# Chunks 5 and 6 rounded behind attention, set differences on VectorE split over the first three steps, sums of weights rounded one a unit from unit 2 on

## The chip, the cores and the metric

The kernel runs on one core of a Trainium2 chip. The metric is the device time of one execution in microseconds (us), as the median of several runs. Engines: TensorE (PE), VectorE (DVE), ScalarE (ACT), GpSimd (POOL), and SyncE (SP), whose queue issues nearly all transfers here.

## What is computed

Retention attention over q, k, v of shape (2, 8, 768, 64), and then two feed-forward layers over the 1536 tokens of width 512, with 2048 hidden features each; the first with SiLU, the second with a leaky ReLU, all in float32:

```python
def _attn_ref(q, k, v):
    gamma = 1.0 - 2.0 ** (-5.0 - np.arange(H))
    for t in range(S):
        state = gamma[None, :, None, None] * state + np.einsum('bhd,bhe->bhde', k[:, :, t], v[:, :, t])
        y[:, :, t] = (1.0 / np.sqrt(D)) * np.einsum('bhd,bhde->bhe', q[:, :, t], state)
def reference(...):
    x = attn_out.transpose(0, 2, 1, 3).reshape(B * S, H * D)
    h = x @ moe_w_in;  x = (h * sigmoid(h)) @ moe_w_out
    h = x @ moe2_w_in; return np.maximum(0.01 * h, h) @ moe2_w_out
```

## The kernel before, in words

**Precision.** Every float32 operand is split into a rounded high half (ScalarE copies it to fp32r) and the rest (VectorE subtracts: L200 and L201 in `halves`). A product is three matmuls: high by high, high by low, low by high. Weights come from DRAM as 64-bit words; `words`, `clamp`, `sign` and `low` make a float32 block of them (ScalarE L144, L146; VectorE L150, L154, L161, L168). The block lies in one of three buffers `r`; `u` holds the low words. A block that is used later is stored to DRAM scratch (`keep_w`, `scr`) and fetched again (`fetch_w`).

**Attention.** Twelve chunks of 128 tokens, two at a time: scores (L266), masked scores on VectorE (L273), values (L283), the product with the state (L295), the outer product (L309) and the new state (L322). `store_x` takes a chunk's result from PSUM and splits it. Three chunks form a set of 384 tokens. Set 0 is split into `xa[0]`, set 1 into a borrowed buffer `b12[0]` and `xb[0]`, sets 2 and 3 likewise for the second pair. The unsplit values stay in `xf` (even sets) and `tm` (odd sets); for the first six chunks (`LATE`) VectorE writes them there scaled, and the split reads them from there. `amid` and `behind` hold the weight work placed inside and after each pair of chunks; `wa`, `wb`, `wc`, `wd` are the first four weight blocks of layer 0.

**Up projections.** Each layer has eight steps (`Q`); a step makes two blocks of 128 hidden features for all tokens. The first two steps of layer 0 and the first of layer 1 are plain products (L878). The others use a seven-product Strassen scheme (`rest`, L394) on token pairs of sets: `first_t` and `rest_t` form the differences of the sets, `split_t` splits them into `T4` (tiles tt), and `sums` forms the sums of weight blocks in `sf`, which `split_s` splits. ScalarE copies partial products out of PSUM (L426) and VectorE adds (L430). `up_tasks` says which helper work is issued ahead of which product. A step's results `g` are kept in DRAM (`keep`, L445); two `big` buffers take turns.

**Down projections.** In layer 0, `fetch_g` (L459) and `split_g` bring g back and `down` (L471) multiplies; each unit is one of the eight pieces of hidden features for one set of 512 tokens. In layer 1 class `Two` does it: units 0 to 7 are plain (L586), the other 32 use seven products (L602) and need the sums of the second weights, which `keep_s` formed in `u` and stored (`scrs`); `ask` fetches them (L576) into `sf` and `u` by turns, and ScalarE and VectorE split them (L648, L654). `third` splits the weights of units 2 to 7 into tiles wt; `high` and `left` (L555, L559) split g.

**Order.** There is no scheduler: the order on each engine, and on SP's transfer queue, is that in which the code issues.

## Time and profile before

| | before |
|---|---|
| median of 3 runs | 560.4 us (559.39 to 563.42) |
| profiled execution | 561.33 us, of which the span is 559.5 us |
| TensorE busy | 542.5 us, 97% of the span |
| VectorE busy | 417.6 us, 75% |
| ScalarE busy | 301.8 us, 54% |
| GpSimd busy | 104.7 us, 19% |
| transfers | 127.54 MB, mean 228 GB/s |

The profile is one execution; times in its rows are microseconds from the start of the span. Busy shares are means over the whole span. Where TensorE waits is read from the list of waits and the timeline. By place: attention runs to about 51 us, the up projection of layer 0 to 173, its down projection to 304, the up projection of layer 1 to 426, and the last stage (class `Two`) to the end.

### The profile page before, as it was taken

Reading aid. Unit: us, or ns where it says so; the run is one execution under the profiler, and the core shown is the slowest. Engines: PE = TensorE matmul, PEld = TensorE weight load, DVE = VectorE, ACT = ScalarE, POOL = GpSimd, SP = SyncE. Lnnn points to the kernel's source line nnn. Section 1 sums busy time; section 2 is a strip of 40 time slices with the busy share of each in tenths; the row PEclk is TensorE's granted clock in tenths of the full one; section 3 lists DMA queues with packets and bytes.
Section 4 is the critical chain, followed back from the end, with each engine's and each line's share of the span. In section 5 each row is a group of like instructions: output and inputs, shape, how many; then the busy total and the mean of one; then the engine's idle time right before and its main releaser. Section 6 shows DMA issues by size and latency. Waiting matters only on the chain.

```text
span 559.5 us, 8890 instructions
## 1 busy us (share of the span) xinstructions
PE 542.5 (97%) x3546; PEld 503.0 (90%) x3546; DVE 417.6 (75%) x546; ACT 301.8 (54%) x367; POOL 104.7 (19%) x92
## 2 busy tenths in 40 slices
PE   7989999999999999999999999998999979999996
PEld 6878999999998788888888999998999858999996
DVE  3798787999956687664867677767877278898993
ACT  2135586777774566644445376646765166443440
POOL 2585322333300000000600662202200000000000
PEclk8999999999999999999999999999999989999999
DMA  8982335778767977889274427776747986642521
GB/s 319 406 336 78 137 127 193 281 266 283 256 227 266 406 237 241 251 289 293 83 255 164 183 114 301 294 293 223 281 150 258 382 311 220 197 136 77 183 82 39
DMA packets 41789, 127.54 MB, mean 228 GB/s; under 512 B 3730, under 2 KB 12050, under 8 KB 39700
## 3 DMA queue, kind: packets, MB, share of 16 engines
q1 hardware_dynamic: 41456, 126.63, 63.8%
q8 instruction: 28, 0.46, 0.3%
q10 hardware_dynamic: 292, 0.34, 0.2%
q14 instruction: 13, 0.11, 0.1%
HBM read 85.01 MB, written 41.94 MB: 227 GB/s over the span
## 4 chain that ended last, share of the span: by engine, by line
PE 58%; DVE 17%; DMA 11%; ACT 5%; issue 5%; POOL 2%; SPq 1%; DVEq 0%; ACTq 0%; POOLq 0%
PE p L394 12%; PE b L394 9%; PE b L602 8%; PE p L471 6%; PE b L471 6%; PE p L602 6%; DMA scr<-r 4%; PE b L878 3%; DVE w L201 3%; DMA c<-g 2%; PE p L878 2%; PE p L586 2%; DVE r L168 2%; PE b L586 2%; DMA sf<-scrs 2%
## 5 line engine op out<-in xcount | busy, mean ns | idle before, releaser
L394 PE MATMUL p<-tt,w 128*128 128x384 f32 x468 | 87.9, 335 | 2.2 <-ACT c L426 2.2
L394 PEld LDWEIGHTS p<-tt,w 128*128 128x128 f32 x468 | 81.8, 188 | 2.9 <-ACT c L426 2.8
L471 PE MATMUL b<-w,wt 128*128 128x512 f32 x216 | 55.1, 390 | 0.5 <-DVE wt L201 0.5
L471 PE MATMUL p<-w,wt 128*128 128x512 f32 x216 | 54.8, 389 | 0.0
L201 DVE TENSOR_TENSOR w<-c,w 128x1024 fp32r<-128x1024 f32 x23 | 29.7, 1293 | 28.9 <-ACT w L200 28.9
L146 ACT ACTIVATE u<-ws 128x1024 int32<-128x1024 uint32 x32 | 36.5, 1139 | 26.3 <-DVE r L168 26.2
L426 ACT ACTIVATE c<-p 128x768 f32<-128x768 f32 x39 | 31.5, 811 | 32.4 <-PE p L394 27.1
L471 PEld LDWEIGHTS b<-w,wt 128*128 128x128 f32 x216 | 40.4, 188 | 9.4 <-DVE wt L201 1.1
L197 POOL TENSOR_TENSOR sf<-r 128x256 f32<-128x256 f32 x26 | 27.7, 1087 | 110.4 <-DVE r L168 59.8
L471 PEld LDWEIGHTS p<-w,wt 128*128 128x128 f32 x216 | 40.5, 188 | 8.4
L161 DVE SCALAR_TENSOR_TENSOR r<-ws,r 128x1024 int32<-128x1024 int32 x32 | 44.3, 1386 | 0.8
L144 ACT ACTIVATE r<-ws 128x1024 f32<-128x1024 f32 x32 | 36.5, 1140 | 13.6 <-DMA scr<-r 7.9
L430 DVE TENSOR_TENSOR big<-b,c 128x384 f32<-128x384 f32 x78 | 39.6, 550 | 5.0 <-ACT c L426 4.6
L168 DVE CUSTOM_DVE_ANT_0 r<-r,u 128x2048 uint16<-128x2048 uint16 x32 | 40.3, 1261 | 0.9
L200 ACT ACTIVATE w<-c 128x1024 fp32r<-128x1024 f32 x23 | 24.4, 1060 | 21.5 <-DMA c<-g 21.5
L201 DVE TENSOR_TENSOR w<-sf,w 128x1024 fp32r<-128x1024 f32 x14 | 17.1, 1225 | 23.3 <-ACT w L200 23.3
L154 DVE TENSOR_SCALAR r<-r 128x1024 int32<-128x1024 int32 x32 | 30.1, 940 | 1.1
L150 DVE TENSOR_SCALAR r<-r 128x1024 f32<-128x1024 f32 x32 | 24.7, 771 | 7.7 <-ACT r L144 7.7
L201 DVE TENSOR_TENSOR w<-r,w 128x768 fp32r<-128x768 f32 (+1 forms) x19 | 22.0, 1159 | 9.9 <-ACT w L200 9.9
L394 PE MATMUL b<-tt,w 128*128 128x384 f32 x156 | 29.2, 335 | 0.0
L394 PE MATMUL p<-xa,w 128*128 128x384 f32 x156 | 29.1, 335 | 0.0
L394 PE MATMUL b<-xb,w 128*128 128x384 f32 x156 | 29.1, 335 | 0.0
(178 smaller groups left out, 1129.7 us busy)
## 6 DMA issues: line engine op xcount, KB each, us to landing
ws<-w_dram SPq DMA_DIRECT2D x64, 512.0 KB, 5.5
g<-big SPq DMA_DIRECT2D x15, 1536.0 KB, 6.9
c<-g SPq DMA_DIRECT2D x30, 512.0 KB, 7.3
att_t<-att_dram SPq DMA_DIRECT2D x20, 512.0 KB, 8.6
scr<-r SPq DMA_DIRECT2D x18, 512.0 KB, 5.9
r<-scr SPq DMA_DIRECT2D x18, 512.0 KB, 5.8
c<-g SPq DMA_DIRECT2D x17, 256.0 KB, 3.4
scrs<-u SPq DMA_DIRECT2D x8, 512.0 KB, 4.0
```

The lines of the kernel that those rows point to most:

```text
L144: nc.scalar.activation(out=r.bitcast(F32), in_=t[:, :, :, 1].bitcast(F32), func=AF.Abs)
L146: nc.scalar.activation(out=u, in_=t[:, :, :, 0].bitcast(U32), func=AF.Copy, scale=2.0 ** -29)
L154: nc.vector.tensor_scalar(out=r, in0=r, scalar1=3, scalar2=0x3FFFFFF8, op0=ALU.logical_shift_left, op1=ALU.bitwise_and,)
L161: nc.vector.scalar_tensor_tensor(out=r, in0=t[:, :, :, 1], scalar=-0x40000000, in1=r, op0=ALU.bitwise_and, op1=ALU.bitwise_or)
L168: nc.vector.tensor_tensor(out=r, in0=r, in1=u, op=ALU.add)
L201: nc.vector.tensor_tensor(out=l, in0=s, in1=h.bitcast(F32), op=ALU.subtract)
L394: nc.tensor.matmul(out=o, lhsT=a[:, ta, k * 128:k * 128 + 128], rhs=rhs(p, tb, k), start=(begin and m == 0), stop=(end and m == 5), skip_g ...
L426: nc.scalar.activation(out=ct[n][:, c, 0:N], in_=t[:, :, 0:N], func=AF.Copy)
L430: nc.vector.tensor_tensor(out=self.block(f, half, c), in0=t[:, :, 0:N], in1=ct[n][:, c, 0:N], op=ALU.add)
L471: nc.tensor.matmul(out=y, lhsT=l, rhs=r, start=(i == 0 and f == 0 and n == 0), stop=(i == Q - 1 and f == 1 and n == 2),)
L602: nc.tensor.matmul(out=y[at][:, 256 * half:256 * half + 256], lhsT=g[:, tg, b], rhs=w[:, tw, a] if sm is None else S[i][tw][:, sm], start= ...
L878: nc.tensor.matmul(out=y[m][0][p][:, 0:N], lhsT=a[:, ta, (A11, A21)[f] + kk // 2, k * 128:k * 128 + 128], rhs=x, start=(i == 0), stop=(i = ...
```

## The change

Six edits. Chunks at positions 4 and 5 (`LATER`, the fifth and sixth) are no longer split in `store_x`, but by `round_x` after the fifth pair of chunks; the clamp of `wb` moves behind the sixth pair. The differences of the sets and the sums of `wc` and `wd` go from GpSimd to VectorE and are dealt out over steps 0 to 2 of layer 0, with `split_t` cut into `high_t` (ScalarE) and `left_t` (VectorE); in step 0 of layer 1 the second half of the differences goes to VectorE too, and one split moves to step 1. `words` can take the buffer `r` given back last. The results of step 6 are kept before the next fetch of g, not after step 7. In layer 1 the last two weight blocks are split before their sums are formed (`direct_s`), and the second piece of g is split one task later. In `Two`, the sums' splits start at unit 2 instead of unit 1, each behind the unit's own work, and the last three are later.

```diff
+LATER = (4, 5)
...
-    def words(w, which=(0, 1)):
+    def words(w, which=(0, 1), at=0):
         t = stage[w]
         if 0 in which:
-            r = rs[w] = rt.pop(0)
+            r = rs[w] = rt.pop(at)
...
-            nc.gpsimd.tensor_tensor(out=o, in0=a, in1=b, op=op)
+            (e or nc.gpsimd).tensor_tensor(out=o, in0=a, in1=b, op=op)
...
+    def high_t(p, n):
+        t = T4[p][:, 2 * n:2 * n + 2]
+        nc.scalar.activation(out=t[:, :, 0], in_=(tm, xf)[n][p], func=AF.Copy)
+
+    def left_t(p, n):
+        t = T4[p][:, 2 * n:2 * n + 2]
+        nc.vector.tensor_tensor(out=t[:, :, 1], in0=(tm, xf)[n][p], in1=t[:, :, 0].bitcast(F32), op=ALU.subtract)
...
     def split_t(p, n):
-        t = T4[p][:, 2 * n:2 * n + 2]
-        halves(t[:, :, 0], t[:, :, 1], (tm, xf)[n][p])
+        high_t(p, n)
+        left_t(p, n)
...
             nc.vector.tensor_tensor(out=f, in0=y, in1=g4(G), op=ALU.mult)
             y = f
+        if j in LATER:
+            return
+        round_x(j, y)
+        if j >= LATE:
+            nc.scalar.activation(out=f, in_=y, func=AF.Copy)
+
+    def round_x(j, y=None):
+        s, c = divmod(j, PER)
+        a, b = c * C, c * C + C
+        if y is None:
+            y = (tm if s % 2 else xf)[s // 2][:, :, :, a:b]
...
+            SUMS = {2: (0,), 3: (1,), 4: (2,), 5: (3,), 6: (4,), 7: (5, 6), 10: (7,)}
+            ASK = {0: (0, 1), 2: (2,), 3: (3,), 4: (4,), 5: (5,), 6: (6,), 7: (7,)}
...
-                if 1 <= n <= Q:
-                    k = n - 1
+                for k in SUMS.get(n, ()):
                     nc.scalar.activation(out=S[k][0], in_=hold[k % 2], func=AF.Copy)
...
-                for k in range(2) if n == 0 else [n + 1] if n + 1 < Q else []:
+                for k in ASK.get(n, ()):
                     ask(k)
...
+        def direct_s(w):
+            t = W[w] = free.pop(0)
+            halves(t[:, 0], t[:, 1], rs[w].bitcast(F32))
+            keep_s(w)
+            rt.append(rs.pop(w))
...
-            nc.gpsimd.tensor_copy(out=gate, in_=l[:, 1, 511:512].bitcast(F32))
...
-            4: lambda: (load_next(), clamp(wb)), 5: lambda: signed(wb),
+            4: lambda: (load_next(), [round_x(j) for j in LATER]), 5: lambda: (clamp(wb), signed(wb)),
...
-                    at(0, lambda: low(wb), lambda: first_t(0, nc.gpsimd), lambda: rest_t(0, nc.gpsimd))
-                    at(1, lambda: words(wc), lambda: split_a(wb))
-                    at(2, lambda: clamp(wc), lambda: signed(wc))
-                    at(3, lambda: low(wc), lambda: sums(wc))
-                    at(4, lambda: split_t(0, 0), lambda: first_t(1, nc.vector))
-                    at(6, lambda: split_t(1, 0))
+                    at(3, lambda: low(wb), lambda: first_t(0, nc.vector))
+                    at(4, lambda: split_a(wb))
+                    at(5, lambda: rest_t(0, nc.vector), lambda: words(wc))
+                    at(6, lambda: clamp(wc), lambda: signed(wc), lambda: low(wc), lambda: split_t(0, 0))
                 else:
-                    at(0, lambda: split_t(0, 1), lambda: rest_t(1, nc.vector))
-                    at(2, lambda: split_a(wc), lambda: words(wd))
-                    at(3, lambda: split_s(wc))
-                    at(4, lambda: split_t(1, 1), lambda: clamp(wd))
-                    at(5, lambda: signed(wd))
-                    at(6, lambda: low(wd), lambda: sums(wd))
+
+                    at(0, lambda: first_t(1, nc.vector), lambda: high_t(0, 1))
+                    at(1, lambda: split_a(wc), lambda: words(wd))
+                    at(2, lambda: high_t(1, 0), lambda: rest_t(1, nc.vector), lambda: left_t(1, 0))
+                    at(3, lambda: sums(wc, nc.vector))
+                    at(4, lambda: left_t(0, 1))
+                    at(5, lambda: split_s(wc))
+                    at(6, lambda: clamp(wd), lambda: signed(wd))
+                    at(7, lambda: high_t(1, 1))
                 return t
             if layer == 0:
+                if k == 2:
+                    at(0, lambda: left_t(1, 1), lambda: low(first_w[3]), lambda: sums(first_w[3], nc.vector))
...
-                    at(4, lambda: (low(b), sums(b)), lambda: words(w, (0,)))
+                    at(4, lambda: (low(b), sums(b)), lambda: words(w, (0,), -1))
...
-                at(0, lambda: fetch_w(n), lambda: first_t(1, nc.vector), lambda: rest_t(1, nc.gpsimd))
+                at(0, lambda: fetch_w(n), lambda: first_t(1, nc.vector), lambda: rest_t(1, nc.vector))
...
-                at(7, lambda: split_t(1, 1), lambda: sums(m))
+                at(7, lambda: sums(m))
                 return t
+            if k == 1:
+                at(0, lambda: split_t(1, 1))
...
-            at(2, lambda: words(w))
+            at(2, lambda: words(w, at=-1))
...
-            at(5, lambda: (low(w), keep_s(w), direct(w) if k > 5 else keep_w(w)))
+            at(5, lambda: (low(w), direct_s(w)) if k > 5 else (low(w), keep_s(w), keep_w(w)))
...
-                    if n:
-                        before.keep()
-                    elif s.layer == 0:
-                        fetch_g(0, 0, 1)
-                    else:
-                        Two.now.fetch(1)
+                    before.keep()
+                    if n is None:
+                        fetch_g(0, 0, 1) if s.layer == 0 else Two.now.fetch(1)
...
-                    tasks[4] += [lambda: two_.fetch(2), lambda: fetch_w((1, 1, 3)), lambda: two_.round(1)]
+                    tasks[4] += [lambda: two_.fetch(2), lambda: fetch_w((1, 1, 3))]
+                    tasks[5] += [lambda: two_.round(1)]
```

TensorE's own order is the same before and after. Three places show how the other engines' orders move. (The numbers behind the names of buffers are handles; lines are those of the kernel named.)

VectorE in attention, from the scaling of the fifth chunk to the new states, before (b_328 and p_364 are PSUM tiles, w_86 and xb_66 hold the split of set 1, c the masked scores):

```order
L363 TENSOR_TENSOR big_69<-b_328,gst 128x2x2x128
L201 TENSOR_TENSOR w_86<-big_69,w_86 128x2x128
L201 TENSOR_TENSOR xb_66<-big_69,xb_66 128x2x128
L273 TENSOR_TENSOR c<-p_364,c 128x1024
L273 TENSOR_TENSOR c<-p_373,c 128x1024
L322 TENSOR_TENSOR gst<-gst,b_391 128x256 x2
```

and after, up to the words of `wa`:

```order
L371 TENSOR_TENSOR big_69<-b_327,gst 128x2x2x128
L273 TENSOR_TENSOR c<-p_363,c 128x1024
L273 TENSOR_TENSOR c<-p_372,c 128x1024
L322 TENSOR_TENSOR gst<-gst,b_386 128x256 x2
L371 TENSOR_TENSOR big_69<-b_336,gst 128x2x2x128
L150 TENSOR_SCALAR r_73<-r_73 128x1024
```

The two passes of L201 between the scaling and the masked scores are gone, and so are the two that stood between the sixth chunk's scaling and L150; all four stand behind the tenth chunk's rounding now.

ScalarE at the start of the last stage, from unit 1's weights on, before (wt are weights of units 2 to 7, gh and w_88 pieces of g, s the sums, which come in sf and u):

```order
L200 ACTIVATE w_89<-r_73 128x1024
L441 ACTIVATE big_68<-big_68 128x2x384
L200 ACTIVATE wt_3548<-r_2584 128x1024
L555 ACTIVATE gh_3563<-c 128x1024
L200 ACTIVATE wt_3548<-r_75 128x1024
L555 ACTIVATE gh_3431<-c 128x1024
L648 ACTIVATE s_3550<-sf 128x1024
L200 ACTIVATE wt_3548<-r_73 128x1024
L555 ACTIVATE w_88<-c 128x1024
L648 ACTIVATE s_3550<-u 128x1024
```

and after:

```order
L200 ACTIVATE w_88<-r_74 128x1024
L572 ACTIVATE w_87<-c 128x1024
L458 ACTIVATE big_68<-big_68 128x2x384
L200 ACTIVATE wt_3546<-r_75 128x1024
L572 ACTIVATE gh_3561<-c 128x1024
L200 ACTIVATE wt_3546<-r_2582 128x1024
L572 ACTIVATE gh_3429<-c 128x1024
L200 ACTIVATE wt_3546<-r_74 128x1024
L572 ACTIVATE w_87<-c 128x1024
L666 ACTIVATE s_3548<-sf 128x1024
```

The first split of sums (from sf) has moved behind the weights and the piece of g of unit 4; unit 1's piece of g stands behind unit 1's weights now.

SP's queue around the same place, before (g_6 is the store of step 6's results, scrs the sums of the second weights, c the fetched pieces of g):

```order
L183 DMA scrs_3399<-u 128x1024
L510 DMA c<-g_1_2827 128x2x512
L187 DMA r_2584<-scr_1_2_2451 128x1024
L510 DMA c<-g_2_2956 128x2x512
L187 DMA r_75<-scr_1_3_2762 128x1024
L183 DMA scrs_3524<-u 128x1024
L445 DMA g_6_3542<-big_69 128x3072
L510 DMA c<-g_3_3085 128x2x512
```

and after:

```order
L183 DMA scrs_3399<-u 128x1024
L462 DMA g_6_3462<-big_69 128x3072
L527 DMA c<-g_1_2825 128x2x512
L187 DMA r_75<-scr_1_2_2449 128x1024
L527 DMA c<-g_2_2954 128x2x512
L187 DMA r_2582<-scr_1_3_2760 128x1024
L183 DMA scrs_3524<-u 128x1024
L527 DMA c<-g_3_3083 128x2x512
```

The store of step 6 stands ahead of the fetch of piece 1 instead of ahead of that of piece 3. Layer 0 has the same exchange.

## Rows read from the trace of the kernel before

**Rows 1.** The page, part 1: busy us, share of the span, instructions.
```profile
PE 542.5 (97%) x3546; PEld 503.0 (90%) x3546; DVE 417.6 (75%) x546; ACT 301.8 (54%) x367; POOL 104.7 (19%) x92
```
**Rows 2.** Waits of TensorE: line and releaser, us in total, times, longest us.
```profile
PE b L283 <- DVE c L273: 2.2, 2, 1.8
PE p L394 <- ACT c L426: 2.2, 2, 1.7
PE p L586 <- ACT w L555: 2.1, 1, 2.1
PE p L586 <- DVE w L559: 1.1, 1, 1.1
...
PE b L471 <- DVE wt L201: 0.5, 1, 0.5
```
**Rows 3.** Timeline of TensorE, last stage: start, us, engine, line, operation.
```profile
426.02 1.54 PE L586 MATMUL p<-w,gh 128*128 128x512 f32 x6
...
442.48 1.53 PE L586 MATMUL p<-wt,gh 128*128 128x512 f32 x6
...
475.06 0.87 PE L602 MATMUL p<-w,gh 128*128 128x256 f32 x6
```
**Rows 4.** Busy time by stretch: length, PE, PEld, DVE, ACT, POOL, clock, DMA.
```profile
448.00:454.00 6.00, 2.74 (x7) 1.92 (x7) 5.67 (x5) 6.00 (x7) 0.00 (x0) 0.79 0.70 230
```
**Rows 5.** VectorE's groups by shape: total us, mean ns, idle before.
```profile
L201 DVE TENSOR_TENSOR xb<-big,xb 128x256 fp32r<-128x256 f32 x4 | 2.5, 624 | 0.0
...
L201 DVE TENSOR_TENSOR w<-big,w 128x256 fp32r<-128x256 f32 x3 | 2.0, 672 | 1.4 <-ACT w L200 1.4
```
**Rows 6.** The same view: the groups that price the first steps.
```profile
L161 DVE SCALAR_TENSOR_TENSOR r<-ws,r 128x1024 int32<-128x1024 int32 x32 | 44.3, 1386 | 0.8
...
L154 DVE TENSOR_SCALAR r<-r 128x1024 int32<-128x1024 int32 x32 | 30.1, 940 | 1.1
...
L201 DVE TENSOR_TENSOR w<-sf,w 128x1024 fp32r<-128x1024 f32 x14 | 17.1, 1225 | 23.3 <-ACT w L200 23.3
...
L201 DVE TENSOR_TENSOR tt<-big,tt 128x1536 fp32r<-128x1536 f32 x8 | 14.5, 1813 | 5.3 <-ACT tt L200 5.3
...
L181 DVE TENSOR_TENSOR u<-r 128x256 f32<-128x256 f32 x16 | 6.1, 422 | 0.3
...
L348 DVE TENSOR_TENSOR big<-big,big 128x768 f32<-128x768 f32 x1 | 1.0, 953 | 0.0
```
**Rows 7.** Timeline of VectorE: the last chunk's last rounding.
```profile
57.11 0.42 DVE L201 TENSOR_TENSOR xb<-b,xb 128x256 fp32r<-128x256 f32 x1 [0.45 <-ACT xb L200]
```
**Rows 8.** Chain that ended last: start, us, what; step 2's first product.
```profile
87.65 2.09 PE p L394 x12
```
**Rows 9.** Timeline of ScalarE in layer 1's up projection, idle before and releaser behind.
```profile
321.80 1.06 ACT L200 ACTIVATE w<-sf 128x1024 fp32r<-128x1024 f32 x1 [3.73 <-POOL sf L197]
...
376.46 1.12 ACT L144 ACTIVATE r<-ws 128x1024 f32<-128x1024 f32 x1 [3.76 <-DMA scr<-r]
```
**Rows 10.** Line L183, the store of u issued at 368.9: its landing.
```profile
DMA to landing us min/median/max: 6.3/6.3/6.3
```
**Rows 11.** Timeline of ScalarE in the last stage.
```profile
447.24 1.06 ACT L648 ACTIVATE s<-sf 128x1024 fp32r<-128x1024 f32 x1 [8.14 <-DMA sf<-scrs]
```
**Rows 12.** Line L187, the fetch of unit 4's weights at 434.5: its landing.
```profile
DMA to landing us min/median/max: 10.0/10.0/10.0
```
**Rows 13.** Line L459, the fetch of piece 1 at 169.0: its landing.
```profile
DMA to landing us min/median/max: 4.2/4.2/4.2
```
**Rows 14.** Timeline of ScalarE and TensorE at the start of layer 0's down projection.
```profile
174.72 1.05 ACT L200 ACTIVATE w<-c 128x1024 fp32r<-128x1024 f32 x1
...
178.36 1.52 PE L471 MATMUL b<-w,w 128*128 128x512 f32 x6
```
**Rows 15.** Line L445, the store of step 6's g at 174.7: its landing.
```profile
DMA to landing us min/median/max: 10.9/10.9/10.9
```
**Rows 16.** Timeline of VectorE at the end of attention.
```profile
51.87 2.22 DVE L154 TENSOR_SCALAR r<-r 128x1024 int32<-128x1024 int32 x1
```

More of the change, by code (lines that the diff above doesn't have):

```diff
@@ L87, in retention_moe_kernel @@
     z1 = sb.tile([128, 1], F32, name="z1")
-    gate = sb.tile([128, 1], F32, name="gate")
     one = sb.tile([1, 64], F32, name="one")
@@ L190, in blocks, with sums @@
         return rs[w].bitcast(F32).rearrange("p a (b n) -> p (a b) n", b=2)
-    def sums(w, which=range(4)):
+    def sums(w, e=None):
         A21, A22, A11, A12 = (blocks(w)[:, n] for n in range(4))
@@ L195, in sums @@
         for o, a, b, op in [((S1, A21, A22, ALU.add), (S3, A11, A21, ALU.subtract),
-                             (S2, S1, A11, ALU.subtract), (S4, A12, S2, ALU.subtract))[n] for n in which]:
-            nc.gpsimd.tensor_tensor(out=o, in0=a, in1=b, op=op)
+                             (S2, S1, A11, ALU.subtract), (S4, A12, S2, ALU.subtract))[n] for n in range(4)]:
+            (e or nc.gpsimd).tensor_tensor(out=o, in0=a, in1=b, op=op)
     def halves(h, l, s):
@@ L369, in store_x @@
             halves(*put(s, a, b, 1)[0:2], y[:, 1])
-        if j >= LATE:
-            nc.scalar.activation(out=f, in_=y, func=AF.Copy)
     TERMS = ((0, 0), (0, 1), (1, 0))
@@ L652, in run @@
                     self.left(n + 2)
-                if 1 <= n <= Q:
+                for k in SUMS.get(n, ()):
                     nc.vector.tensor_tensor(out=S[k][1], in0=hold[k % 2], in1=S[k][0].bitcast(F32), op=ALU.subtract)
-                for k in range(2) if n == 0 else [n + 1] if n + 1 < Q else []:
+                for k in ASK.get(n, ()):
                     ask(k)
@@ L802, in up_tasks @@
                 if k == 0:
-                    at(0, lambda: low(wb), lambda: first_t(0, nc.gpsimd), lambda: rest_t(0, nc.gpsimd))
-                    at(1, lambda: words(wc), lambda: split_a(wb))
-                    at(2, lambda: clamp(wc), lambda: signed(wc))
-                    at(3, lambda: low(wc), lambda: sums(wc))
-                    at(4, lambda: split_t(0, 0), lambda: first_t(1, nc.vector))
-                    at(6, lambda: split_t(1, 0))
-                else:
-                    at(0, lambda: split_t(0, 1), lambda: rest_t(1, nc.vector))
-                    at(2, lambda: split_a(wc), lambda: words(wd))
-                    at(3, lambda: split_s(wc))
-                    at(4, lambda: split_t(1, 1), lambda: clamp(wd))
-                    at(5, lambda: signed(wd))
-                    at(6, lambda: low(wd), lambda: sums(wd))
+                    at(3, lambda: low(wb), lambda: first_t(0, nc.vector))
+                    at(4, lambda: split_a(wb))
+                    at(5, lambda: rest_t(0, nc.vector), lambda: words(wc))
+                    at(6, lambda: clamp(wc), lambda: signed(wc), lambda: low(wc), lambda: split_t(0, 0))
+                else:
+                    at(0, lambda: first_t(1, nc.vector), lambda: high_t(0, 1))
[6 more added lines that the diff above has]
+                    at(7, lambda: high_t(1, 1))
                 return t
             if layer == 0:
+                if k == 2:
+                    at(0, lambda: left_t(1, 1), lambda: low(first_w[3]), lambda: sums(first_w[3], nc.vector))
                 if k + 1 < Q:
                     a = first_w[k + 1]
-                    at(0, lambda: split_a(a))
-                    at(1, lambda: split_s(a))
+                    at(int(k == 2), lambda: split_a(a))
+                    at(1 + int(k == 2), lambda: split_s(a))
                 w = second_w[0][k - 2]
@@ L951, in retention_moe_kernel @@
                 rest(s, n, steps[k - 1], tasks)
-            steps[Q - 2].keep()
             steps[Q - 1].act(0, 1)
```

## The prediction

> **What bounds the kernel now.** The page's busy shares come first: TensorE is busy for 97% of the span, VectorE for 75%, GpSimd for 19% [rows 1]. The change leaves TensorE's instruction order as it is and removes no matmul, so what it can give back is TensorE's idle time, and what slower matmuls behind an idle stretch cost. I therefore read the waits of TensorE next [rows 2]: who it waited for, the total, how often, the longest. Five waits matter. The values product of attention (L283) waits for the masked scores of VectorE (L273), 1.8 us in one piece. The Strassen products (L394) wait twice for ScalarE's copy out of PSUM (L426), 1.7 and so 0.5 us. The last stage (L586) waits 2.1 us for a rounded piece of g on ScalarE and 1.1 us more for its low half on VectorE. The first down stage (L471) waits 0.5 us. That is 7.7 us of waiting.
>
> The last stage costs more than its waits. In the timeline its unit 0 (units are counted from 0) starts at 426.02 and unit 3 at 442.48, so a unit takes 5.49 us and eight take 43.9; the next phase starts at 475.06, 49.04 after the first [rows 3]. The excess is 5.1 us, 3.2 of it the waits. The rest is slow matmuls: after the idle stretch the granted clock is 0.79 on the mean from 448 to 454 us [rows 4], that is, TensorE was put from 2.4 to 1.2 GHz for part of it.
>
> **The change part by part, in the order of the program.**
>
> *Chunks 5 and 6.* Four VectorE roundings leave the attention stage, at 0.67 and 0.62 us mean; the group also shows 1.4 us of waiting for ScalarE over three chunks, so 0.47 each [rows 5]. Two chunks are 2 x (0.67 + 0.62 + 0.47) = 3.5 us. They stand ahead of the masked scores that TensorE waits 1.8 us for, so that wait goes. The lower bound is 0 (VectorE reaches the scores before TensorE has made them), the upper 2.2, if its lead takes away as much as both waits of that row of rows 2. What is late next: the following masked scores, since TensorE now comes 1.8 us earlier and VectorE has its 3.5 us to meet that with. I take 1.7. The rounding comes back before the last two chunks are stored, 4 x about 0.42 us (the smaller passes of the same kind are below the means above), beside the first two products of step 0, which read only xa[0]. It is hidden there.
>
> *Set differences, splits and the weights' sums on VectorE.* GpSimd loses six set differences and the eight small sums of the first steps; VectorE gets them, and its order becomes a single chain from the last chunk of attention to the sums of the second weight block (wc), which step 2's first product needs. I price it by group means [rows 6]: two groups of word passes at no more than 0.94 + 0.94 + 1.39 + 1.39 = 4.66 us, 9.3; eight set differences at 0.95, 7.6; three low halves of tt at 1.81, 5.4; four sums at 0.42, 1.7; three low halves of weights at 1.23, 3.7. Together 27.7 us. It starts where the last chunk's rounding ends, 57.11 + 0.42 before [rows 7], some 1.7 earlier now: 55.8. So it ends at 83.5. TensorE begins that product at 87.65 before [rows 8], so at about 85.9 now. The margin is 2.4 us and I cost the part at nothing; if the cover goes, each us beyond 2.4 is a us of TensorE. The DMA queues keep their order here; the third block's words are asked for by signed(wb), right after attention as before.
>
> *First weights of the second layer.* With the differences of set pair 1 on VectorE, GpSimd is free for the sums of the first Strassen block, for which ScalarE waited 3.7 us before it could come to the copy that held TensorE [rows 9]. This is the 0.5 us wait; it goes.
>
> *words(w, at=-1).* It takes the buffer given back last instead of the one that is still being stored. In the second layer ScalarE stood 3.8 us before L144 for that store [rows 9], with L146, L441 and the copy L426 behind it: this is the 1.7 us wait. What ends last now is the store of u, which L146 overwrites: issued at 368.9, landed 6.3 later, at 375.2 [rows 10], 2.4 us before the 376.46 + 1.12 at which L146 could start. So the copy comes 2.2 to 2.4 us earlier and 1.7 goes. Lower bound 0, if that store takes longer in the new order.
>
> *Last stage.* ScalarE waited 8.1 us for the sums' transfer before it rounded them, and only then came to unit 4's weights and piece of g that TensorE stood idle for [rows 11]. Now the first sums come one unit later and behind both. What is late next is unit 4's own weights: asked for at 434.5 and landed 10.0 later, 444.5 [rows 12]. Two ScalarE passes (1.06 each, as the one in rows 11) and one VectorE pass (1.23, as the low half of this size in rows 6) behind it end at 447.9; the unit starts at 426.02 + 4 x 5.49 = 447.98. So the stall goes even with the old queue, and with g of step 6 stored a step earlier 1.5 MB less stand ahead of these weights. The order of ScalarE shows no other wait ahead of a unit. I take all 5.1 us, and 0 as the other bound. The last sum, rounded at unit 10, is one VectorE pass of 1.2 us in a phase where VectorE rounds two units ahead: at nothing. So is the new order at the start of the stage (unit 1's weights rounded before their sums are formed, unit 1's piece of g after them): these are the same passes, and unit 1 starts 5.49 us after unit 0.
>
> *Keeping g of step 6 before the next fetch, both layers.* In the first layer this takes 1.5 MB from in front of the pieces for unit 3, where TensorE waits 0.5 us; that wait goes. It puts them in front of unit 1's piece, which is the second rival.
>
> **Sum.** 1.7 + 0.5 + 0.5 + 1.7 + 5.1 = 9.5 us. The profiled execution took 561.3 us (span 559.5), so 551.8; the median of the runs is 0.9 below it. What was removed is waiting, and part of the 0.9 may be waiting of that one execution, so I take a third of it off and say 551.5.
>
> **Rivals.**
> *A. The last stage keeps its stall in another place.* Unit 4 has 0.1 us to spare by the old landing; if the earlier keep moves nothing forward, or the transfers of the next weights, which share the queue with the sums, are late, TensorE falls idle and the clock with it. Price up to 5.1: 556.6. Against it: 1.5 MB less are under way. Chance 0.12.
>
> *B. The keep delays unit 1.* In the first layer the fetch landed 4.2 us after its issue at 169.0 [rows 13]; ScalarE took it up at 174.72 and unit 1 began at 178.36 [rows 14]. The keep of step 6, in the crowded stretch where it stood before, took 10.9 us [rows 15]. If the fetch lands only with such a keep, it is 6.7 us later, at 179.9, 5.2 after 174.72; ScalarE and VectorE take 1.05 and 1.2 (done at 177.1, so 1.2 to spare), which leaves a stall of 4.0: 555.5. For it: both go through SP's one queue. Against it: that keep took 10.9 with weight loads ahead of it, and here it goes first into queues that have little to do. The Trainium skill speaks against the change here: "DMA: Bandwidth & Descriptors", section on queues, rings and completion order, says that each DMA engine takes the pieces of one queue in ring order, so the fetch would stand behind all of the keep. No row here shows the two queued so. By that rule, with a keep as slow as that one, the time is 555.5; by the row alone, where the fetch needed 4.2, it is 551.5. Chance 0.10.
>
> *C. Attention gives nothing.* VectorE is ahead, but the next masked scores or GpSimd's scaling of the queries hold TensorE instead: 551.5 + 1.7 = 553.2. Chance 0.10.
>
> *D. Slower: VectorE becomes the bound of the first three steps.* The 27.7 us chain meets its end with 2.4 to spare. A pass can cost far more than its mean: L154 took 2.22 us at 51.87 [rows 16], 2.4 times its mean. If the whole chain ran at 1.8 times its price, 50 us, TensorE would stand 20 us at step 2 and the time be 571; slower than before by 1% it is from 14.5 us of delay, a chain of 45 us. The 2.22 came beside GpSimd's differences, and the new order gives GpSimd nothing to do there until the fifth weight block's sums. Chance 0.04.
>
> **How the numbers follow.** The forecast has 0.64, A 0.12, B 0.10, C 0.10, D 0.04; its own range is 549.5 to 554. For the range I go down to 548.5 (the other 0.5 of the attention bound, the rest of the 0.9, and as much as the runs spread in their faster half) and up to 556.6, A in full; D and a little on either side stay out. One per cent, about what a measurement of this kernel can tell from no change, is 5.6 us: faster means below 554.8. The forecast, C and half of B lie there, 0.79; the rest of B and A are within 1%, 0.17; D is slower.
>
> **What would show it.** In the profile after: no wait of L283 for L273 above 0.5 us, and the first L878 near 49.8; no wait of L394 for ScalarE's copy; the last stage 44 us long from its first unit to the 256-column matmuls, at a granted clock of 1.00; no VectorE wait of TensorE at step 2, with the wc sums' low half ended before TensorE's product at about 86. The prediction is wrong if TensorE shows a new wait over 1 us: for VectorE between 60 and 100 us (D), for unit 1's piece in either layer (B), or for a transfer in the last stage (A).

## The result, and the profile of the changed kernel

The changed kernel takes 553.08 us in the median of 4 runs (552.97 to 554.74), beside 561.66 for the kernel before on the same chip: a ratio of 0.9856 with a 95% interval of 0.981 to 0.9902. On a second chip it was 551.82 (550.91 to 552.71) beside 559.74, again 0.9856, interval 0.9839 to 0.9873, that is 7.1 to 9.0 us less. The forecast was 551.5, in a range of 548.5 to 556.6. The profiled execution took 552.97, its span 551.2; that of before was 561.33 and 559.5, while the median of before on the three chips used later was 559.2 to 560.0. That execution of before had a mean granted clock of 0.992; of the 49 runs of before on those three chips, nine had 0.998 and took 557.0 to 559.2.

The waits of TensorE in the profile after (line and releaser, us in total, times, longest; L411 was L394, L443 was L426, L488 was L471, L603 was L586); three that stand in the profile of before too are left out:

```profile
PE p L411 <- ACT big L458: 0.7, 1, 0.7
PE b L488 <- DVE wt L201: 0.6, 1, 0.6
PE b L309 <- POOL att_w L249: 0.5, 1, 0.5
PE b L283 <- DVE c L273: 0.4, 1, 0.4
PE p L411 <- ACT c L443: 0.4, 1, 0.4
```

Against [rows 2], the 1.8 us piece for L273, the 1.7 for ScalarE's copy and both waits of the last stage are gone. The wait of the first down stage is still there, 0.6 us instead of 0.5, and 0.7 for ScalarE's activation L458, 0.5 for GpSimd's keys (L249) and 0.4 for a copy at another place (165 us) are new. The prediction had said that no wait for ScalarE's copy would be left; that sign failed, without harm to the forecast. The stretch behind unit 4 of the last stage, to be set beside [rows 4] (clock third from the end):

```profile
450.00:460.00 10.00, 10.00 (x45) 8.03 (x44) 9.22 (x14) 5.44 (x6) 0.00 (x0) 1.00 0.81 262
```

Where the stages begin on TensorE, first before (the last stage is in [rows 3]), then after:

```profile
51.55 4.46 PE L878 MATMUL p<-xa,w 128*128 128x384 f32 x24
172.88 1.55 PE L471 MATMUL b<-w,w 128*128 128x512 f32 x6
304.34 2.28 PE L878 MATMUL p<-xa,w 128*128 128x384 f32 x12
```

```profile
47.46 4.45 PE L905 MATMUL p<-xa,w 128*128 128x384 f32 x24
169.77 1.52 PE L488 MATMUL b<-w,w 128*128 128x512 f32 x6
301.46 2.25 PE L905 MATMUL p<-xa,w 128*128 128x384 f32 x12
421.97 1.55 PE L603 MATMUL p<-w,gh 128*128 128x512 f32 x6
466.28 0.87 PE L619 MATMUL p<-w,gh 128*128 128x256 f32 x6
```

| stage, us | before | after | change |
|---|---|---|---|
| attention | 51.55 | 47.46 | -4.09 |
| up, layer 0 | 121.33 | 122.31 | +0.98 |
| down, layer 0 | 131.46 | 131.69 | +0.23 |
| up, layer 1 | 121.68 | 120.51 | -1.17 |
| last stage, units 0 to 7 | 49.04 | 44.31 | -4.73 |
| what follows unit 7 | 84.44 | 84.92 | +0.48 |

Two things stand out: attention gave far more than 1.7 us, and three stages became longer, and the waits in them account for only a part of it. The experiments follow these two, and then ask which of the predicted terms were real.

### The profile page after: what moved, and what is told of

Read it like the earlier page. It is cut to its first block, busy times and chain, and to the rows that moved or that the text cites. A ratio compares the mean times of both kernels' runs of the same rounds, so it can differ in the third digit from the quotient of the medians.

```text
span 551.2 us, 8864 instructions
## 1 busy us (share of the span) xinstructions
PE 540.6 (98%) x3546; PEld 502.5 (91%) x3546; DVE 418.8 (76%) x560; ACT 303.3 (55%) x367; POOL 82.3 (15%) x77
## 4 chain that ended last, share of the span: by engine, by line
PE 80%; DVE 8%; DMA 7%; issue 2%; ACT 2%; SPq 0%; DVEq 0%; ACTq 0%
PE p L411 19%; PE b L411 14%; PE b L619 8%; PE p L488 7%; PE b L488 7%; PE p L619 6%; PE p L603 4%; PE b L603 4%; PE b L905 3%; PE p L905 3%; DMA att_t<-att_dram 3%; DMA scr<-r 2%; DMA c<-g 1%; DVE w L201 1%; DVE r L168 1%
## 5 line engine op out<-in xcount | busy, mean ns | idle before, releaser
L411 PE MATMUL p<-tt,w 128*128 128x384 f32 x468 | 88.3, 336 | 0.4 <-ACT c L443 0.4
L411 PEld LDWEIGHTS p<-tt,w 128*128 128x128 f32 x468 | 82.3, 188 | 0.8 <-ACT c L443 0.7
L488 PE MATMUL b<-w,wt 128*128 128x512 f32 x216 | 55.3, 390 | 0.6 <-DVE wt L201 0.6
L488 PE MATMUL p<-w,wt 128*128 128x512 f32 x216 | 54.9, 389 | 0.0
L443 ACT ACTIVATE c<-p 128x768 f32<-128x768 f32 x39 | 31.6, 810 | 41.2 <-PE p L411 33.9
L201 DVE TENSOR_TENSOR w<-c,w 128x1024 fp32r<-128x1024 f32 x23 | 29.7, 1293 | 29.0 <-ACT w L200 29.0
L488 PEld LDWEIGHTS b<-w,wt 128*128 128x128 f32 x216 | 40.4, 188 | 9.6 <-DVE wt L201 1.1
L488 PEld LDWEIGHTS p<-w,wt 128*128 128x128 f32 x216 | 40.5, 188 | 8.5
L197 POOL TENSOR_TENSOR sf<-r 128x256 f32<-128x256 f32 x22 | 21.2, 984 | 168.2 <-DVE r L168 70.2
L201 DVE TENSOR_TENSOR w<-sf,w 128x1024 fp32r<-128x1024 f32 x14 | 17.1, 1225 | 24.5 <-ACT w L200 24.5
L411 PE MATMUL p<-xa,w 128*128 128x384 f32 x156 | 29.4, 337 | 0.7 <-ACT big L458 0.7
L411 PE MATMUL b<-tt,w 128*128 128x384 f32 x156 | 29.4, 336 | 0.0
L411 PE MATMUL b<-xb,w 128*128 128x384 f32 x156 | 29.3, 337 | 0.0
L411 PE MATMUL b<-xa,w 128*128 128x384 f32 x156 | 29.3, 337 | 0.0
L411 PEld LDWEIGHTS p<-xa,w 128*128 128x128 f32 x156 | 27.3, 188 | 1.0 <-ACT big L458 1.0
L154 DVE TENSOR_SCALAR r<-r 128x1024 int32<-128x1024 int32 x32 | 27.2, 850 | 1.1
```

The costliest lines, as they stand in the source:

```text
L201: nc.vector.tensor_tensor(out=l, in0=s, in1=h.bitcast(F32), op=ALU.subtract)
L411: nc.tensor.matmul(out=o, lhsT=a[:, ta, k * 128:k * 128 + 128], rhs=rhs(p, tb, k), start=(begin and m == 0), stop=(end and m == 5), skip_g ...
L443: nc.scalar.activation(out=ct[n][:, c, 0:N], in_=t[:, :, 0:N], func=AF.Copy)
L488: nc.tensor.matmul(out=y, lhsT=l, rhs=r, start=(i == 0 and f == 0 and n == 0), stop=(i == Q - 1 and f == 1 and n == 2),)
```

## Experiments

Each kernel is the changed one with the edit shown, or before where it says so. Ratios are to the kernel before on the same chip.

### The changed kernel again

> The changed kernel a second time, to be compared with the next three on the same chip, and to see what the first 15 us do from one execution to another. In the profile before, the granted clock fell to 0.50 from 11 to 14 us after TensorE had waited 1.15 us for a transfer, and in the profile after it stayed at 1.00 after a wait of 1.08. Theory 1 (this is the execution, not the change): the median is again near 553, and the first plain product begins at 47.5 us if the clock stays at 1.00 and near 49.2 if it falls. Theory 2 (the change does it): always 47.5.

It took 551.82, as given above; its first plain product begins at 47.30. Its profile has one wait that the first one shows smaller (0.4):

```profile
165.93 2.37 PE L411 MATMUL p<-tt,w 128*128 128x384 f32 x12 [1.00 <-ACT c L443]
```

It does not need the change: the kernel of the run sums_alone below, which has the code of before there, shows it too, with 0.57 at 171 us.

What differs at the start is the clock (third number from the end), in before and in the changed kernel; the run keep_late below is like before, with 0.51:

```profile
12.00:14.00 2.00, 2.00 (x37) 2.00 (x35) 0.44 (x1) 0.00 (x0) 0.59 (x1) 0.50 1.03 416
```

```profile
12.00:14.00 2.00, 2.00 (x48) 1.93 (x45) 0.36 (x2) 0.00 (x0) 0.80 (x1) 1.00 1.03 420
```

and what TensorE did before it fell, in before and in keep_late, with keep_late's first plain product:

```profile
5.26 1.16 PE L266 MATMUL p<-att_t 64*128 64x128 f32 x16 [0.48 <-DMA att_t<-att_dram]
```

```profile
5.17 2.39 PE L266 MATMUL p<-att_t 64*128 64x128 f32 x32 [0.69 <-DMA att_t<-att_dram]
...
48.44 4.45 PE L905 MATMUL p<-xa,w 128*128 128x384 f32 x24
```

In 5 of the 13 profiles of this study the first scores waited 0.48 to 0.69 us for their transfer, and in exactly these the clock is at 0.50 to 0.51 from 12 to 14 us; this is called the slow start below. In the other 8 they waited at most 0.19 and it stays at 1.00, though a wait of 0.6 to 1.3 us before L283 at 10 us is in all 13. Kernels with the new attention are in both groups (2 with the slow start, 8 without), so theory 2 fell; they begin step 0 at 48.4 to 48.7 and at 47.1 to 47.9. The three profiles with chunks 5 and 6 rounded at once all have the slow start; nothing in the code ahead of 12 us differs, but three are few. About 1.0 of the 4.09 us came from this start (48.44 in keep_late beside 47.46 in the changed kernel). No run set this first wait on purpose, so that it is what makes the clock fall is not shown.

### The place of the operands: 32 and 64 bytes of room

```diff
     z1 = sb.tile([128, 1], F32, name="z1")
+    gap = sb.tile([128, 1], F32, name="gap")
```

and, in the second run, this as well:

```diff
     cs = sb.tile([128, ncs], F32, name="cs")
+    gap0 = sb.tile([128, 1], F32, name="gap0")
```

> The changed kernel with one more tile of 4 bytes that nothing uses, where the tile gate had been. The change dropped gate, and with it every tile allocated behind it (tt, wt, the slots w) begins 32 bytes earlier than before, while xa, xb, big, c and gh stay. In the profile after, a Strassen step takes 14.68 us instead of 14.58, all the way through, and the products from 466 us on about 0.4 us more in all. Theory 1 (the place of the matmul operands in memory sets this): a step takes 14.58 again and the time falls by 1.5 to 2 us against the changed kernel. Theory 2 (VectorE's and ScalarE's new order slows the matmuls): the step stays at 14.68 and the time does not move.

> As the run with 32 bytes of room, with 32 bytes more ahead of xa. All operands of the matmuls then begin at a multiple of 64 bytes. Before, all began 32 bytes behind one; in the changed kernel xa, xb and gh begin 32 behind one and w, tt and wt at one. Theory 1a (two operands that lie differently are what costs): 14.58 us a Strassen step, as with 32 bytes of room. Theory 1b (the weights' own place costs): 14.68 a step, as in the changed kernel. Theory 2 (not the place): 14.68 in both runs with room.

The same group of 12 matmuls in two successive Strassen steps: before, in the changed kernel, with 32 and with 64 bytes of room (L412 and L413 are L411 there):

```profile
99.99 2.24 PE L394 MATMUL b<-xb,w 128*128 128x384 f32 x12
...
114.57 2.24 PE L394 MATMUL b<-xb,w 128*128 128x384 f32 x12
```

```profile
95.74 2.25 PE L411 MATMUL b<-xb,w 128*128 128x384 f32 x12
...
110.42 2.25 PE L411 MATMUL b<-xb,w 128*128 128x384 f32 x12
```

```profile
95.73 2.24 PE L412 MATMUL b<-xb,w 128*128 128x384 f32 x12
...
110.31 2.24 PE L412 MATMUL b<-xb,w 128*128 128x384 f32 x12
```

```profile
95.97 2.24 PE L413 MATMUL b<-xb,w 128*128 128x384 f32 x12
...
110.55 2.24 PE L413 MATMUL b<-xb,w 128*128 128x384 f32 x12
```

A step takes 14.68 us in the changed kernel and 14.58 in both others, and 14.58 before; the engines' orders are the same in all three changed ones. So tiles of 4 bytes that nothing uses take the 0.1 us away, and of the three theories only 1a fits: operands that lie differently cost, not the weights' own place. The places themselves are worked out from the order in which the code makes its tiles; no trace shows an address, and which pair of tiles it is was not tried. The later stages show it too: with 32 bytes of room units 0 to 7 of the last stage take 43.81 us and what follows 84.51, where the changed kernel's second profile has 44.31 and 84.88. With six steps in layer 0 at 0.1 each and the new wait of 0.36 us there, this is nearly all of what the up projection of layer 0 and the end of the kernel grew by. The times fell by less than the rows: 550.98 (550.45 to 551.56) and 551.36 (550.35 to 551.99) beside 551.82, that is 0.8 and 0.5 us where 13 steps alone make 1.3, and the runs overlap. Where the rest of it goes stays open.

### The last stage: order of the sums, place of the store

Old order of sums in the changed kernel:

```diff
-            SUMS = {2: (0,), 3: (1,), 4: (2,), 5: (3,), 6: (4,), 7: (5, 6), 10: (7,)}
-            ASK = {0: (0, 1), 2: (2,), 3: (3,), 4: (4,), 5: (5,), 6: (6,), 7: (7,)}
+            SUMS = {k + 1: (k,) for k in range(Q)}
+            ASK = {0: (0, 1), **{k - 1: (k,) for k in range(2, Q)}}
```

> The changed kernel with the weights' sums of the last stage asked for and rounded one unit earlier again, as before, all else as changed. Theory 1 (that order is what held TensorE: ScalarE stands at the sums' transfer ahead of unit 4's weights): the waits of L603 for g on ScalarE and VectorE come back, 2 to 3.2 us, the clock falls in the stretch behind them, the stage from its first unit to the 256-column matmuls takes 48 to 49.5 us instead of 44.3, and the time rises by 4 to 5. Theory 2 (the earlier store of step 6 and the later rounding of the second piece of g are enough): the stage stays under 45 and the time within 1 us.

ScalarE's first sums, and the stretch behind unit 4 (busy time by engine, clock, DMA):

```profile
439.39 1.06 ACT L666 ACTIVATE s<-sf 128x1024 fp32r<-128x1024 f32 x1 [6.64 <-DMA sf<-scrs]
```

```profile
448.00:454.00 6.00, 6.00 (x28) 4.86 (x27) 3.79 (x4) 2.96 (x3) 0.00 (x0) 1.00 1.01 397
```

ScalarE stands at the sums again (6.64 us, 8.14 in [rows 11]), but they land 17.1 us after unit 0's start instead of 21.2, and TensorE waits for nothing. The stage took 44.30 us: theory 1 fell as it was put. The time was 553.27 (ratio 0.9879, 0.9863 to 0.9895); its profiled execution has the slow start, which explains that one, not the median 1.4 above the changed kernel; that is open, and the intervals of the two ratios overlap.

The order of the sums alone, in the kernel before (the run sums_alone; the four places of SUMS and ASK as in the change):

> The kernel before with one part of the change alone: the weights' sums of the last stage are asked for and rounded in the new order; the store of step 6 stays behind step 7. With the old order of sums but the early store (the run sums_old) the stage had no stall: 44.3 us. Theory 1 (either part is enough; unit 4's weights landed at 444.5 before, and two passes of ScalarE and one of VectorE behind them end 0.1 us before the unit's start at 447.98): the waits of L586 go, the stage takes 43.9 to 44.5 us, the time falls by 4.5 to 5 against before. Theory 2 (only the early store is enough, since the fetches of weights and of g stand behind 3 MB of stores): a wait of 0.5 to 3 us stays at unit 4 or 5, the stage takes 45 to 49, and the time falls by 0 to 4.

```profile
455.27 1.43 PE L586 MATMUL p<-wt,gh 128*128 128x512 f32 x5 [0.95 <-DVE gh L559]
```

```profile
451.76 1.06 ACT L200 ACTIVATE wt<-r 128x1024 fp32r<-128x1024 f32 x1 [2.85 <-DMA r<-scr]
```

555.9 us beside 559.23, ratio 0.9933 (0.991 to 0.9956). The stage took 45.12 us (426.49 to 471.61): unit 4 no longer waits, unit 5 waits 0.95 for its piece of g, which ScalarE rounded only behind unit 5's weights, and for these it had stood 2.85 us. Theory 2, at its mild end.

Both old, the sums as in the first diff of this part, and:

```diff
-                    before.keep()
-                    if n is None:
+                    if n or s.layer == 0:
+                        before.keep()
+                    if n is None:
...
+            if layer:
+                steps[Q - 2].keep()
             steps[Q - 1].act(0, 1)
```

> The changed kernel with both the old order of the sums and the old place of the store of step 6 in the second layer; the later rounding of the second piece of g and the earlier split of the last two weight blocks stay. With either alone in the new way the stage had a wait of 0.95 (new sums, old store) or none (old sums, new store). Theory 1 (these two are the causes, each enough or nearly): the waits of L603 for g come back, 2 to 3.2 us in all, the stage takes 47.5 to 49.5 us instead of 44.3, the time rises by 3.5 to 5. Theory 2 (a third part of the change freed it): the stage stays under 45.5 and the time rises by less than 1.2.

```profile
444.47 0.50 PE L603 MATMUL p<-wt,w 128*128 128x512 f32 x1 [1.25 <-ACT w L572]
...
446.11 1.49 PE L603 MATMUL p<-wt,w 128*128 128x512 f32 x5 [1.13 <-DVE w L576]
```

```profile
448.00:454.00 6.00, 6.00 (x22) 4.78 (x21) 4.37 (x5) 3.17 (x4) 0.00 (x0) 0.77 0.98 357
```

The stall is back in unit 4 with the slow clock behind it (0.77), the stage takes 48.88 us, the time is 557.1, ratio 0.9945 (0.9919 to 0.997), 0.0089 or 5.0 us above the changed kernel's. Theory 1 holds. So the stall had two causes, and taking away one is nearly enough: the earlier store wholly, within the rest of the change, and the order of the sums in the kernel before but for 0.95 us.

### Chunks 5 and 6 rounded at once

```diff
-LATER = (4, 5)
+LATER = ()
```

> The changed kernel with chunks 5 and 6 rounded at once again. Theory 1 (the roundings are what made the masked scores late): the wait of L283 for L273 near 38 us comes back, 1.5 to 2 us, and the first plain product of step 0 begins 1.8 to 2.3 us later than in the changed kernel, at 49.1 to 49.8 with the clock at 1.00 throughout (1.4 to 1.7 later still where the clock falls at 11 us); the time rises by 1.8 to 2.3. Theory 2 (the 4.1 us by which attention ended earlier came from the start of that execution alone): under 0.5 us.

```profile
41.95 1.97 PE L283 MATMUL b<-c,att_t 128*64 128x128 f32 x16 [2.50 <-DVE c L273]
43.71 1.57 PE L283 MATMUL b<-c,att_w 128*64 128x128 f32 x16
...
54.48 4.43 PE L905 MATMUL p<-xa,w 128*128 128x384 f32 x24
```

The stretch around it here, and the same group of products in the profile of before:

```profile
36.00:44.00 8.00, 5.50 (x92) 5.06 (x90) 7.97 (x9) 1.24 (x3) 5.63 (x5) 0.84 0.39 159
```

```profile
40.08 1.09 PE L283 MATMUL b<-c,att_t 128*64 128x128 f32 x16 [1.81 <-DVE c L273]
```

Theory 1, and larger than it said: the wait is back with 2.50 us, the granted clock is 0.84 over the stretch, and the two groups of 16 products behind the wait take 1.97 and 1.57 us. In before they took 1.09 each, at a clock of 1.00: the clock did not fall behind the wait of 1.81 us there, and fell behind this one and behind the 2.04 us of sums_alone (0.83), which also rounds at once. Step 0 begins 6.0 us later than in the profile of keep_late, which has the same slow start; in before it was 3.1 later and in sums_alone 4.8. That execution was a long one; the median is 554.94, ratio 0.9918 (0.9888 to 0.9948), 0.0062 or 3.5 us above the changed kernel; from the two intervals I put the uncertainty at 1.9 either way.

### words at the oldest buffer

```diff
-            at(2, lambda: words(w, at=-1))
+            at(2, lambda: words(w))
```

> The changed kernel with words of the second layer taking the oldest buffer again. Theory 1 (ScalarE stands at the store of that buffer, and the copy of PSUM behind it): the wait of the Strassen product for ScalarE's copy near 370 to 380 us comes back, 1.5 to 1.9 us, and the time rises by as much. Theory 2 (the earlier rounding of the last two weight blocks and the new order of the stores freed it): no wait above 0.5 there and no change of time.

```profile
370.93 1.14 ACT L144 ACTIVATE r<-ws 128x1024 f32<-128x1024 f32 x1 [0.97 <-DMA scr<-r]
```

ScalarE waits 0.97 us for the store, not 3.76 as in [rows 9], and TensorE has no wait for the copy there. 552.73 us, ratio 0.9866 (0.9834 to 0.9897). By this profile theory 1 fell; the ratio alone, 0.6 us above the changed kernel's, could not tell 1.7 from nothing. Theory 2 is not needed either: the kernel with the order of the sums alone has the code of before in this stage, and its profile shows the store waited for only 1.19 us and no wait of TensorE:

```profile
376.27 1.13 ACT L144 ACTIVATE r<-ws 128x1024 f32<-128x1024 f32 x1 [1.19 <-DMA scr<-r]
```

Nor does it show the 0.5 us wait of the first Strassen step of that layer (at 323.99 us before). So of two executions of this code one has both waits and the other neither; how often they come is not known.

### The store of step 6 in the first layer

```diff
-                    before.keep()
+                    if n or s.layer:
+                        before.keep()
...
+            if layer == 0:
+                steps[Q - 2].keep()
             steps[Q - 1].act(0, 1)
```

> The changed kernel with the store of step 6 of the first layer behind step 7 again; the second layer as changed. In the changed kernel L488 waits 0.6 us at unit 2 for weights that ScalarE splits behind unit 2's piece of g, which landed 7.8 us after its issue; before it waited 0.5 at unit 3. Theory 1 (the 1.5 MB of the store push the transfers behind it back, and the wait only changed its unit): the wait at unit 2 goes, one of about 0.5 comes back at unit 3, the time stays within 0.5 us. Theory 2 (the two weight loads issued ahead of unit 2's piece are what makes it late): 0.5 to 0.7 us stay at unit 2 and a second wait may come at unit 3, the time is 0 to 0.6 longer.

TensorE's wait in the changed kernel (169.77 is unit 0), and in keep_late (unit 0 at 170.43):

```profile
182.02 1.21 PE L488 MATMUL b<-w,wt 128*128 128x512 f32 x4 [0.64 <-DVE wt L201]
```

```profile
188.12 1.21 PE L488 MATMUL b<-w,wt 128*128 128x512 f32 x4 [0.51 <-DVE wt L201]
...
194.37 1.21 PE L488 MATMUL b<-w,wt 128*128 128x512 f32 x4 [0.46 <-DVE wt L201]
```

Unit 2's wait goes, units 3 and 4 get one of 0.5 each; 552.49 us, ratio 0.9864 (0.9831 to 0.9896). Theory 1: the early store only moves the wait.

### Four more passes of VectorE

```diff
-                    at(6, lambda: clamp(wc), lambda: signed(wc), lambda: low(wc), lambda: split_t(0, 0))
+                    at(6, lambda: clamp(wc), lambda: signed(wc), lambda: low(wc), lambda: split_t(0, 0), *[lambda: left_t(0, 0)] * 4)
```

> The changed kernel with the low half of set pair 0's first difference formed five times over instead of once in step 0 (the same values each time): 4 x 1.75 = 7.0 us more of VectorE in the chain from attention's last rounding to the sums of wc. In the profile after that chain ends at 78.01 and TensorE comes to its product at 83.18. Theory 1 (the margin is 5.2 us, and VectorE stood 0.4 us in the chain): TensorE waits 1.4 to 1.8 us for VectorE at that product, the time rises by 1.4 to 2 (more if the clock falls behind it). Theory 2 (the margin is the 2.4 us of the prediction): 4 to 4.6 us. Theory 3 (the chain is not what that product waits for): no wait and no change.

VectorE, ScalarE and TensorE:

```profile
65.01 8.93 DVE L357 TENSOR_TENSOR tt<-big,tt 128x1536 fp32r<-128x1536 f32 x5
...
78.32 1.75 DVE L357 TENSOR_TENSOR tt<-big,tt 128x1536 fp32r<-128x1536 f32 x1
```

```profile
80.17 0.81 ACT L456 ACTIVATE big<-p 128x768 f32<-128x768 f32 x1 [2.08 <-DVE tt L357]
```

```profile
81.03 3.79 PE L411 MATMUL p<-xa,w 128*128 128x384 f32 x12 [2.24 <-ACT big L456]
```

None of the three as put. TensorE waits earlier than theory 1 says, at the first Strassen product (78.98 us in the changed kernel, not 83.18): ScalarE's activation, which frees its PSUM, writes step 1's results over set differences that VectorE has still to split. VectorE reached that split 7.2 us later against TensorE (78.32 for 71.49, with everything ahead 0.35 earlier) and made 2.24 of wait, so the margin is about 4.9 us. The 12 products behind it took 3.79 us instead of 2.25. The time is 556.81, ratio 0.9933 (0.9907 to 0.9959), 0.0077 or 4.3 us above the changed kernel, of which 3.8 are these two.

### Four edits together

```diff
+    gap = sb.tile([128, 1], F32, name="gap")
...
-                at(0, lambda: fetch_w(n), lambda: first_t(1, nc.vector), lambda: rest_t(1, nc.vector))
-                at(1, lambda: split_t(1, 0))
+                at(0, lambda: fetch_w(n), lambda: first_t(1, nc.vector))
+                at(1, lambda: split_t(1, 0), lambda: rest_t(1, nc.vector))
...
-                    tasks[4] += [lambda: fetch_g(layer, 0, 2), lambda: fetch_w(ahead[1]), lambda: split_g(layer, 0, 1)]
+                    tasks[4] = [lambda: fetch_g(layer, 0, 2)] + tasks[4] + [lambda: fetch_w(ahead[1]), lambda: split_g(layer, 0, 1)]
...
-                    tasks[4] += [lambda: fetch_g(0, 0, 0) if layer == 0 else Two.fetch_first()]
+                    tasks[2 if layer == 0 else 4] += [lambda: fetch_g(0, 0, 0) if layer == 0 else Two.fetch_first()]
```

> The changed kernel with four edits that the runs so far point to: the 4 byte tile as in the run with 32 bytes of room; unit 2's piece of g of the first layer asked for ahead of the step's two weight loads; the first piece of that stage asked for two tasks earlier; and in step 0 of the second layer the second half of the set differences on VectorE behind the first split of their set instead of ahead of it. Theory 1 (each takes away what was measured): 0.8 us from the place of the operands, the wait of 0.6 at unit 2, the wait of 0.4 to 1.0 for ScalarE's copy near 165 us that three of five profiles of kernels with this order show, and the 0.7 near 316 that one shows: 1.5 to 2.5 us less than the changed kernel, a ratio to the kernel before of 0.981 to 0.983 where the changed kernel has 0.9856. Theory 2 (the transfers moved forward push others back): a wait of 0.5 or more at unit 3 or for the weights there, and a ratio of 0.984 as with the 32 bytes alone.

```profile
PE p L412 <- ACT c L444: 0.6, 2, 0.3
...
PE p L412 <- DVE w L202: 0.4, 1, 0.4
```

549.72 us (549.35 to 550.94), ratio 0.981 (0.9772 to 0.9847). No wait is left in the first down stage. The wait in step 0 of the second layer is 0.4 us, now for VectorE's low half of the weights, and two of 0.3 for the copy came near 134 and 138 us. It is the fastest kernel here, 2.1 us below the changed one in the median, as theory 1 has it; they ran on different chips and their intervals overlap, so that much is likely rather than shown.

## Why the prediction was right, and where not

**Last stage, 5.1 us: right, with half its cause.** The stage fell by 4.73 in the profiles (by 5.23 with the 32 bytes of room), and undoing both parts costs 5.0. The sentence that the stall goes even with the old queue was nearly right: it left 0.95 us at unit 5, whose weights still came late. The earlier store, which the prediction named second, takes the whole stall away without the new order of the sums.

**Attention, 1.7 us: mechanism right, size too small.** Undoing it costs 3.5 us. The upper bound of 2.2 was the sum of two waits. It left out the delays around the long one: like with like (slow start), step 0 begins at 51.55 in before and at 48.44 in keep_late, 3.1 us, of which 2.0 are the long wait, 0.6 stand one pair of chunks earlier (at about 31 us) and 0.4 right behind the wait. It also left out the slow products that followed the wait in two other executions, 1.97 us instead of 1.09 with the chunks rounded at once. What was late next, in the first profile, was GpSimd's keys, 0.5 us; none of the nine other profiles with the new attention lists that wait. Its two passes took 2.02 us beside VectorE's sign and low passes, one of which took 2.23:

```profile
37.57 2.23 DVE L161 SCALAR_TENSOR_TENSOR r<-ws,r 128x1024 int32<-128x1024 int32 x1
```

```profile
38.68 2.02 POOL L249 TENSOR_TENSOR att_t<-att_t,cs 128x512 f32<-128x512 f32 x1
```

Such a pass of VectorE takes 1.23 us where GpSimd is idle (62.85 us), and the two of GpSimd took 1.04 each in the profile of before, beside other work of VectorE. The Trainium skill, "SBUF — State Buffer", section "SBUF: two separate sides", says that VectorE, in a pass with two inputs from SBUF, and GpSimd shut each other out of a shared port pair for a whole instruction; these rows, where both passes are longer side by side, agree.

**words at the last buffer, 1.7, and the first weights of the second layer, 0.5: not borne out.** Both waits were real in [rows 2] and [rows 9] but are absent from another profile of the same code. The step that failed is the one from one execution to the sum: 0.9 us between the profile and the median was noticed, and only 0.3 of it taken off. In the changed profile the place of the second had another wait, 0.7 for L458, which the repeated run does not show either.

**First down stage, 0.5: wrong.** The store in front gained one fetch and delayed another. This is rival B at a sixth of its price, one unit later. The store took 6.0 us instead of the 10.9 of [rows 15]; unit 1's piece, issued 1.5 us behind it, landed in 5.9, at 172.1, when ScalarE had just become free. The Trainium skill's rule that the prediction cited for B ("DMA: Bandwidth & Descriptors", "Queues, rings and completion order") puts the fetch behind the store; this trace agrees, the fetch landed 1.4 us behind it. So B had the queue right and the store's time wrong. The next piece was the late one, 7.8 us, and ScalarE waited 2.24 for it:

```profile
178.51 1.07 ACT L200 ACTIVATE w<-c 128x1024 fp32r<-128x1024 f32 x1 [2.24 <-DMA c<-g]
```

**VectorE's chain at no cost: right, with the wrong end.** It took 25.2 us instead of 27.7, from 52.8 to 78.0. The margin is 4.9, not 2.4, and lies at the first Strassen product, through the buffer of step 1's results, which the prediction did not look at. The last row of that chain:

```profile
76.78 1.23 DVE L201 TENSOR_TENSOR w<-sf,w 128x1024 fp32r<-128x1024 f32 x1 [0.40 <-ACT w L200]
```

**Not seen at all:** the removed tile of 4 bytes, listed in the diff, made every Strassen step 0.1 us longer; putting it back took that away.

By the undone parts, the change is 3.5 + 5.0 - 0.8 = 7.7 us; 7.9 was measured on the second chip, closer than the intervals of the parts can promise. That the forecast of 551.5 came so near 551.82 is luck, since errors stood against each other: 2.7 us too much for three small waits and 0.8 for the unseen tile on one side, 1.8 too little for attention on the other, and a start from 561.3 where the median of before is 559.7.

## What to carry to other kernels

A wait in one profile is a sample: before pricing its removal, look for it in a second execution, and take the profile's excess over the median off the sum first. Price a wait of TensorE with the slow products behind it, and ask of a delayed engine which buffer is overwritten next, not only who reads its result. When a tile is dropped or added, look where the tiles behind it begin.

## What the hardware showed that was not expected

- With the tiles that the matmuls read at different places (by the order of the code, xa, xb and gh 32 bytes behind a multiple of 64, w, tt and wt at one) the 84 matmuls of a Strassen step took 14.68 us; with all at either place, 14.58.
- A wait of 0.48 to 0.69 us for the first transfer, at 5 us, goes with a clock of 0.50 to 0.51 at 12 to 14 us (5 profiles); in the other 8 the longer wait at 10 us leaves the clock at 1.00.
- The same wait for the masked scores was followed by a granted clock of 1.00 in one execution (1.81 us, before) and of 0.83 and 0.84 over 36 to 44 us in two others (2.04 us, sums_alone; 2.50 us, chunks at once).
